# A fused attention, feed-forward and soft-MoE kernel: sign bits taken by GpSimd, the last weights loaded in whole rows, extra matmuls whose result nobody reads, and a new sequence

## The chip, the cores and the metric

The kernel runs on one core of a Trainium2 chip. The metric is the device time of one execution in microseconds (us). The core has five engines that each work through a queue of their own in order: TensorE (PE in the profile; its weight loads stand as PEld), VectorE (DVE), ScalarE (ACT), GpSimd (POOL) and SyncE (SP, which only issues transfers here). An instruction waits on semaphores for the results that it needs and for the buffer that it writes. SBUF is the memory that all engines work in, PSUM the one that matmuls write to.

## The reference

Three computations follow on one another. Only the last one's result leaves the kernel.

```python
# clustered attention: B=2, H=8, S=768, D=64, 16 clusters
q_assign = argmax(normalised q . normalised centroids); k_assign likewise
mask   = q_assign[:, :, :, None] == k_assign[:, :, None, :]
scores = where(mask, q k^T / sqrt(D), -1e9)
attn   = softmax(scores) @ v                       # as 1536 tokens x 512
# feed-forward: 512 -> 2048 -> 512
h = x @ w_in;  g = h * clip(h + 3, 0, 6) / 6;  y = g @ w_out
# soft MoE: 8 experts x 4 slots, F = 1024
logits = y @ phi
d = softmax(logits, over tokens);  slot_input = d.T @ y
slot_out[e] = maximum(slot_input[e] @ w1[e], 0) @ w2[e]     # 4 rows each
out = softmax(logits, over slots) @ slot_out                # 1536 x 512, float32
```

The feed-forward weights `w_in` and `w_out` arrive as float64; the other inputs are float32.

## The kernel before

One function holds everything. Each piece of work is a Python generator that `ev(...)` appends to a list: a piece issues a few instructions and yields. A string of numbers, `ORDER` (2,600 of them), says which generator is stepped next, and `flush` steps them in that order. This order is the program order, and so the order in every engine's queue. A second table, `ROOMS`, says for each tile name which of the buffers of its kind ("rooms") it takes. There are three PSUM rooms of two banks for scores and most other products (`pss`) and two of one bank (`psm`).

The stages, with the times of the profiled execution of before:

- **0 to 31 us, start.** Constants, centroids, and head 0: q and k are loaded, cast to a high and a low float16 half (L330 to L341) and transposed by PE (L382, tile `tq`); the other heads' transposes are made by a DMA. Then cluster assignment (`as_mm`, L428) and row maxima.
- **31 to 136 us, the eight heads of the first batch.** For each head and each of six blocks of 128 rows: scores for the row maximum (`sm`, PE L514), the maximum (`mxs`, DVE L530), scores again (`st`, PE L552 and L556), the exponential (`p`, ACT L600), its float16 halves (`pp`, ACT L331 and POOL L341) and the product with v (`acc`, PE L622 to L628). Between these stands the narrowing of the float64 weights: eight tiles of 128x1024 of `w_in` (`win`) and eight of `w_out` (`wout`).
- **136 to 320 us.** The second batch's heads, interleaved with the feed-forward of the first six token tiles (`hid`, PE L693, and `act`), its logits and the dispatch to slots.
- **320 to 405 us.** The feed-forward of the other six token tiles.
- **405 us to the end at 473.7 us.** The slots: the experts' first layer (`layer1`, PE L1324), relu, a transpose, the second layer (`layer2`, PE L1361, for experts 0 to 3, and `layer2_part`, PE L1381, for experts 4 to 7, the "last group"), `slots_out` (PE L1278), and `combine` (PE L1305, evictions L1311 and L1313), which writes the output with DMAs (L1315).

**The narrowing.** A float64 value is two 32-bit words. `narrow` builds the float32 in three parts: part 0 takes the sign bit of the high word (DVE L861, tile `nw`, one buffer) and, on ACT, the absolute value scaled (L863, tile `nt` in a `pss` room); part 1 shifts and joins both (DVE L866); part 2 joins the top bits of the low word (DVE L871). DVE and ACT have other work between these parts.

**The loads of the last phase.** `fetch` takes the entries of a list, `chunks`, one after another; each issues two or more DMAs on SP: "o" is the product `w_out` written back to memory, "1" the experts' first weights, "2" the second weights of experts 0 to 3 in halves of four row blocks, and "d" the second weights of experts 4 to 7 in column parts, `PARTS` being columns 0 to 255, 256 to 383 and 384 to 511. The column parts let the last phase run column by column: as soon as the first part's weights are there, its second layer, its `slots_out` and its `combine` can run and its output can leave, while the next part's weights load.

## Time and profile before

| | before |
|---|---|
| time, median of 3 runs | 481.71 us (479.29 to 484.8) |
| the profiled execution's own time | 475.53 us |
| its span, first to last instruction | 473.7 us |
| PE busy | 427.5 us (90% of the span) |
| ACT busy | 316.9 us (67%) |
| DVE busy | 283.1 us (60%) |
| POOL busy | 248.8 us (53%) |
| bytes moved by DMA | 95.48 MB, mean 202 GB/s |
| granted TensorE clock, mean | 0.987 |

The profiled execution is itself shorter than the three timed ones; the rows below add up to its 475.53 us, of which 1.8 us lie outside the span. A busy share of 90% for PE is a mean over stages with different limits, and PE's matmuls are pipelined with modelled ends. The chain that ended last is followed back from the last instruction, so each of its entries delayed what stands behind it. The DMA share is that of the core's 16 DMA engines, and can pass 1 where packets overlap.

### The profile page before, as it was taken

What the parts mean: (1) busy time and instruction counts of PE and PEld (TensorE: products, weight loads), DVE (VectorE), ACT (ScalarE), POOL (GpSimd) and SP (SyncE); (2) the same over time, 40 slices, a digit from 0 to 9 for tenths busy, and PEclk for the clock granted to TensorE, in tenths of its full rate; (3) what the DMA queues carried; (4) which work ended last, traced back from release to release, by engine and by line L of the source; (5) the groups of instructions that cost most, each with busy time, mean ns of one, the idle gap of its engine ahead of it and who ended that gap; (6) DMA issues with size and microseconds to landing.
All of it is one profiled execution on the core that took longest, in us unless ns stands there. A gap on an engine that the chain in (4) does not pass through costs nothing.

```text
span 473.7 us, 11606 instructions
## 1 busy us (share of the span) xinstructions
PE 427.5 (90%) x4802; PEld 271.8 (57%) x4802; DVE 283.1 (60%) x497; ACT 316.9 (67%) x518; POOL 248.8 (53%) x227
## 2 busy tenths in 40 slices
PE   2699999999979999999999998989898999889884
PEld 1357677777857466656666666654554444533353
DVE  4999999999957576375666868422244124631123
ACT  5699998899966779767889898963355336500121
POOL 4467658757534466576788897983322333030000
PEclk9999999999989999999999999999999999979999
DMA  8788959756779854584858956008998769998998
GB/s 263 212 158 213 264 102 286 167 157 229 189 242 221 182 147 86 90 136 113 179 125 127 149 119 125 1 1 135 282 412 293 167 142 342 409 396 293 345 291 274
DMA packets 133812, 95.48 MB, mean 202 GB/s; under 512 B 96384, under 2 KB 119424, under 8 KB 133760
## 3 DMA queue, kind: packets, MB, share of 16 engines
q1 hardware_dynamic: 129088, 88.95, 72.3%
q10 hardware_dynamic: 4672, 5.80, 3.5%
q8 instruction: 37, 0.61, 0.6%
q14 instruction: 15, 0.12, 0.1%
HBM read 64.06 MB, written 7.34 MB: 151 GB/s over the span
## 4 chain that ended last, share of the span: by engine, by line
PE 50%; DVE 18%; ACT 11%; DMA 8%; issue 6%; POOL 5%; DVEq 0%; ACTq 0%; SPq 0%; POOLq 0%
PE h L693 21%; DVE mxs L530 7%; PE e L1324 3%; ACT p L600 3%; PE st L552 3%; PE st L556 3%; POOL pp L341 2%; PE sm L514 2%; PE acc L622 2%; ACT pp L331 2%; POOL ghl L341 2%; DMA wk<-in_moe_w_dram 2%; DMA wod<-in_moe_w_out_dram 2%; PE z L802 1%; PE o L1361 1%
## 5 line engine op out<-in xcount | busy, mean ns | idle before, releaser
L341 POOL TENSOR_TENSOR pp<-p,pp 128x768 f16<-128x768 f32 x72 | 118.6, 1655 | 56.0 <-ACT pp L331 23.4
L693 PE MATMUL h<-wq,xt 128*128 128x512 f16 x576 | 131.6, 379 | 1.1 <-DMA xt<-xhl 1.1
L530 DVE TENSOR_REDUCE mxs<-sm 128x1 f32<-128x768 f32 x96 | 88.9, 952 | 16.5 <-PE sm L514 15.8
L693 PEld LDWEIGHTS <-xt 128*128 128x128 f16 x576 | 55.2, 98 | 62.1 <-DMA xt<-xhl 2.0
L341 POOL TENSOR_TENSOR ghl<-r,ghl 128x1024 f16<-128x1024 f32 (+1 forms) x25 | 50.3, 2012 | 61.5 <-ACT ghl L331 57.4
L600 ACT ACTIVATE p<-st 128x768 f32<-128x768 f32 x72 | 57.9, 808 | 13.2 <-PE st L556 9.8
L331 ACT ACTIVATE pp<-p 128x768 f16<-128x768 f32 x72 | 60.4, 844 | 1.2
L552 PE MATMUL st<-qk1t 128*128 128x384 f16 x192 | 48.4, 334 | 5.6 <-ACT p L600 4.0
L712 DVE SCALAR_TENSOR_TENSOR r<-r,h 128x1024 f32<-128x1024 f32 (+1 forms) x26 | 29.6, 1137 | 38.7 <-ACT r L710 38.6
L514 PE MATMUL sm<-qk2t 80*128 80x384 f16 x192 | 47.2, 339 | 4.6 <-DVE qk2t L385 1.5
L556 PE MATMUL st<-qk2t 102*128 102x384 f16 x192 | 48.7, 335 | 0.0
L710 ACT ACTIVATE r<-h,b_relu 128x1024 f32<-128x1024 f32 (+1 forms) x26 | 27.2, 1046 | 24.3 <-PE h L693 17.0
L627 PE MATMUL acc<-v,pp 128*128 128x65 f16 x432 | 36.1, 192 | 0.2 <-DVE mv L501 0.2
L622 PE MATMUL acc<-v,pp 128*128 128x65 f32 x288 | 36.2, 276 | 0.0
L628 PE MATMUL acc<-v,pp 128*128 128x64 f16 x432 | 36.1, 194 | 0.0
L622 PEld LDWEIGHTS acc<-v,pp 128*128 128x128 f32 x288 | 35.3, 195 | 1.2 <-DVE mv L501 0.3
L331 ACT ACTIVATE ghl<-r 128x1024 f16<-128x1024 f32 (+1 forms) x26 | 25.7, 988 | 14.9 <-DVE r L712 10.9
L627 PEld LDWEIGHTS <-pp 128*128 128x128 f16 x432 | 31.1, 99 | 3.3 <-DVE mv L501 0.6
L341 POOL TENSOR_TENSOR qk<-qk,qk 128x768 f16<-128x768 f32 x15 | 24.7, 1645 | 13.5 <-DMA qk<-in_q_dram 4.8
L628 PEld LDWEIGHTS <-pp 128*128 128x128 f16 x432 | 29.2, 96 | 2.7
L331 ACT ACTIVATE qk<-qk 128x768 f32<-128x768 f32 (+2 forms) x32 | 26.0, 818 | 3.7 <-DMA qk1t<-qk 2.5
L552 PEld LDWEIGHTS <-qk1t 128*128 128x128 f16 x192 | 17.3, 103 | 17.3 <-issue 11.4
(193 smaller groups left out, 756.3 us busy)
## 6 DMA issues: line engine op xcount, KB each, us to landing
wk<-in_moe_w_dram SPq DMA_DIRECT2D x60, 512.0 KB, 8.2
wi<-in_moe_w_in_dram SPq DMA_DIRECT2D x16, 512.0 KB, 6.1
wod<-in_moe_w_out_dram SPq DMA_DIRECT2D x16, 512.0 KB, 5.0
wos<-wo ACTq DMA_DIRECT2D x8, 512.0 KB, 4.3
wk<-wos SPq DMA_DIRECT2D x8, 512.0 KB, 5.5
qk<-in_q_dram SPq DMA_DIRECT2D x16, 192.0 KB, 3.3
qk<-in_k_dram SPq DMA_DIRECT2D x16, 192.0 KB, 3.4
v<-in_v_dram SPq DMA_DIRECT2D x16, 192.0 KB, 3.7
```

Source lines behind the costliest of these rows:

```text
L331: nc.scalar.activation(out, in_, AF.Copy, scale=scale)
L341: (nc.vector if e == "v" else nc.gpsimd).tensor_tensor(out=out, in0=in_, in1=hi, op=ALU.subtract)
L514: nc.tensor.matmul(s[:, j, 0:384], d["qk2t"][0:80, n, 0], d["qk2t"][0:80, 3 * j : 3 * j + 3, 1], start=True, stop=True,)
L530: nc.vector.tensor_reduce(out=mxs[i % 2][:, 96 + n : 97 + n], in_=s[:, :, 0:384], op=ALU.max, axis=AX.XY)
L552: nc.tensor.matmul(s[:, j, 0:384], d["qk1t"][:, t, 1], d["qk1t"][:, 3 * j : 3 * j + 3, 0], start=True, stop=False)
L556: nc.tensor.matmul(s[:, j, 0:384], d["qk2t"][0 : 96 + NT, t, 1], d["qk2t"][0 : 96 + NT, 3 * j : 3 * j + 3, 0], start=False, stop=True,)
L600: nc.scalar.activation(p32, s[:, :, 0:384], AF.Exp, scale=sc_exp)
L622: nc.tensor.matmul(o, p32[:, j, r * P : (r + 1) * P], d["v32"][:, t], start=(t == 0 and n == 0), stop=False)
L627: nc.tensor.matmul(o, hi, v1[:, t, 0:65], start=(t == 0 and n == 0), stop=False)
L628: nc.tensor.matmul(o[:, 0:64], hi, v1[:, t, 65:129], start=False, stop=False)
L693: nc.tensor.matmul(s[:, fb % 2], xt[:, lhs], wq[fb][:, hl, kk], start=(n == 0), stop=(n == 11))
L712: nc.vector.scalar_tensor_tensor(out=g, in0=r, scalar=6.0 * SG, in1=sf, op0=ALU.min, op1=ALU.mult)
```

## The change

1. **The sign on GpSimd.** In `narrow`, part 0's sixteen DVE instructions become POOL instructions: the high word, read as a float32, times 0.0, which is a zero with the word's sign. The `nw` tile still has one buffer. Part 1 on DVE now waits for POOL.
2. **Extra matmuls.** `keep(n, m)` makes m matmuls of 128x256 float16 from constants into a `pss` tile that is read by nobody: 77 pieces and 168 matmuls. The first 47 pieces (108 matmuls) stand in the first 164 of `ORDER`'s 2,758 steps, nine (18 matmuls) at the end of the second batch's heads, five (10) in the slot phase, and 16 (32) behind the last matmul of the output.
3. **The last group's second layer.** Of the eight row blocks (c) of experts 4 to 7, blocks 0 to 3 are loaded as ordinary "2" chunks and blocks 4 and 5 as "c" chunks, whole rows of 512 columns, and multiplied by `layer2_rows` for all three column parts. Only blocks 6 and 7 are still loaded and multiplied by column part (`layer2_part`). All in one group, the sums grow in one `psm` and one `pss` tile, `op`.
4. **Small things.** The last token tile's `pe` takes a `pss` room; `slots_out` yields between its two matmuls; and `ORDER` and `ROOMS` are new throughout. The order of the last three parts is now columns 0 to 255, 384 to 511, 256 to 383.

The tables are cut to a line.

```diff
-    "1 1 2 8 2 8 9 9 0 9 1 9 9 9 9 1 0 5 5 3 5 13 13 1 10 10 10 10 11 11 14 15 5 0 9 795 796 6 796 797 103 103 798 "
+    "9 9 8 8 15 0 0 814 15 16 16 811 831 812 805 2 808 835 12 12 12 0 0 12 16 837 816 807 16 16 7 810 8 8 10 20 11 "
...
+    def keep(n, m):
+        t = pss(f"kw_{n}")
+        for _ in range(m):
+            nc.tensor.matmul(t[:, 0, 0:256], ident16, ident.bitcast(F16), start=True, stop=True)
+        yield
...
-        pe = psm(f"pe_{t}")
+        pe = psm(f"pe_{t}") if t < NTOK - 1 else pss(f"pe_{t}")[:, 0]
...
-            nc.vector.tensor_scalar(out=s, in0=hi, scalar1=0x80000000, scalar2=None, op0=ALU.bitwise_and)
+            sf = s.bitcast(F32)
+            nc.gpsimd.tensor_scalar(out=sf, in0=hi.bitcast(F32), scalar1=0.0, scalar2=None, op0=ALU.mult)
...
-    chunks += [("d", E - 4 + j, 0) for j in range(4)] + [("d", E - 4, 1)]
+    chunks += [("2", E - 4 + j, 0) for j in range(4)]
+    chunks += [("c", E - 4, 0), ("c", E - 2, 0), ("d", 0, 0), ("d", 1, 0)]
...
+        if kind in ("c", "d"):
+
+            t = room(n, rooms[n], 2048, f"wk_{n}")
+            if kind == "c":
+                t = t.rearrange("p (j c d) -> p j c d", j=2, c=2)
+                for j in range(2):
+                    src = w2[e + j].rearrange("(p c) d -> p c d", c=8)
+                    nc.sync.dma_start(t[:, j], src[:, 4:6])
+                    wt_[kind, e + j] = t[:, j]
+                    yield
+                return
             for p, (c0, w) in enumerate(PARTS):
-                if p:
-                    np = 2 if p == 2 else 1
-                    for c in range(np):
-                        cc = slice(8 // np * c, 8 // np * (c + 1))
-                        for j in range(4):
-                            src = w2[e + j].rearrange("(p c) d -> p c d", c=8)
-                            nc.sync.dma_start(ts[j][:, p - 1, cc], src[:, cc, c0 : c0 + w])
-                            yield
+                if (p > 0) != (e > 0):
+                    continue
+                tp = t[:, 1024 * (p == 2) :][:, 0 : 8 * w].rearrange("p (c j d) -> p c j d", j=4, c=2)
+                wt_["d", p] = tp
+                for c in range(2):
+                    src = w2[E - 4 :].rearrange("e (p c) d -> c p e d", c=8)[6 + c]
+                    nc.sync.dma_start(tp[:, c], src[:, :, c0 : c0 + w])
+                    yield
             return
-        elif kind == "d":
-            src = w2[e].rearrange("(p c) d -> p c d", c=8)[:, :, 0:256]
...
     ev(consts)
+    for n in range(7):
+        ev(keep, n, 4)
...
+    for n in range(40):
+        ev(keep, 7 + n, 2)
...
+    def layer2_rows(i):
+        g = NG - 1
+        if i == 0:
+            sl["op", 0] = psm("op_0")
+            t = pss("op_1")
+            sl["op", 1], sl["op", 2] = t[:, 0], t[:, 1]
+        for c in (range(4), range(4, 6))[i]:
+            for p, (c0, w) in enumerate(PARTS):
+                for j in range(4):
+                    wr = wt_["c", E - 4 + j][:, c - 4] if i else wv("2", E - 4 + j, 0, c)
+                    nc.tensor.matmul(
+                        sl["op", p][32 * j : 32 * j + 32, 0:w], hw(g, c, j), wr[:, c0 : c0 + w], start=(c == 0), stop=False
+                    )
+            if i == 0 and c % 2:
+                yield
+        yield
+
+    def layer2_part(p):
         c0, w = PARTS[p]
-        if i == 0:
-            sl["o2", NG - 1, p] = psm(f"o2_{NG - 1}_{p}")
-        for c in range(4 * i, 4 * i + 4):
+        for c in range(6, 8):
             for j in range(4):
                 nc.tensor.matmul(
-                    sl["o2", NG - 1, p][32 * j : 32 * j + 32, 0:w],
+                    sl["op", p][32 * j : 32 * j + 32, 0:w],
                     hw(NG - 1, c, j),
-                    wv("d", E - 4 + j, p, c)[:, 0:w],
-                    start=(c == 0),
+                    wt_["d", p][:, c - 6, j],
+                    start=False,
                     stop=(c == 7),
                 )
...
+    for n in range(30):
+        ev(keep, 47 + n, 2)
...
+    for i in range(2):
+        ev(layer2_rows, i)
     for p in range(len(PARTS)):
-        for i in range(2):
-            ev(layer2_part, p, i)
+        ev(layer2_part, p)
```

How the change moves instructions, at three places. First DVE's queue of before, within the first batch's heads: the sign of the first half of the second block of `w_in` (`nw_i`) between row maxima (`mxs`), with the cluster assignment (`as`, `mx`) behind it.

```order
L530 TENSOR_REDUCE mxs_114<-sm_1_467 128x1
L530 TENSOR_REDUCE mxs_114<-sm_4_479 128x1
L861 TENSOR_SCALAR nw_i_0_484<-wi_0_305 128x1024
L530 TENSOR_REDUCE mxs_114<-sm_3_486 128x1
L530 TENSOR_REDUCE mxs_114<-sm_0_497 128x1
L530 TENSOR_REDUCE mxs_114<-sm_5_501 128x1
```

In the changed kernel this sign stands in POOL's queue (lines are shifted, L341 is L354 there), among the low halves of v, of q and k, and of the probabilities (`pp`).

```order
L354 TENSOR_TENSOR pp_1_617<-p_0_1_618,pp_1_617 128x768
L354 TENSOR_TENSOR v_2_109<-v_2_112,v_2_109 128x6x64
L881 TENSOR_SCALAR nw_i_0_751<-wi_0_439 128x1024
L354 TENSOR_TENSOR qk_4_724<-qk_659,qk_4_724 128x6x128
L354 TENSOR_TENSOR pp_3_634<-p_0_3_635,pp_3_634 128x768
L881 TENSOR_SCALAR nw_i_1_840<-wi_1_747 128x1024
L354 TENSOR_TENSOR pp_5_757<-p_0_5_758,pp_5_757 128x768
```

Behind it on DVE the instruction that waits for POOL's sign is L886, which was L866.

```order
L558 SCALAR_TENSOR_TENSOR qk2t_615<-sm_5_655,nident 6x6x128
L471 TENSOR_TENSOR as_670<-as_670,rank 128x12x16
L886 SCALAR_TENSOR_TENSOR nt_i_0_750<-nt_i_0_750,nw_i_0_751 128x1024
L474 TENSOR_REDUCE mx_3_784<-as_670 128x12
L476 TENSOR_TENSOR oh_786<-as_670,mx_3_784 128x6x2x16
L891 SCALAR_TENSOR_TENSOR wi_0_439<-wi_0_439,nt_i_0_750 128x1024
```

The sign has left DVE; the two joining steps have stayed, with two instructions of a cluster assignment between them and more such work behind.

The second place is PE's queue at the program's start. Before, it opened with the transposes of head 0's q and k.

```order
L1450 UNCONDITIONAL_BRANCH
L382 LDWEIGHTS qk_0_132
L382 MATMUL tq_155<-ident_86,qk_0_132 128x128
L382 LDWEIGHTS qk_0_132
L382 MATMUL tq_155<-ident_86,qk_0_132 128x128
```

Now 24 matmuls of `keep` stand ahead of them; these rows are the last of these and the first transposes (L401 was L382).

```order
L363 MATMUL kw_207<-ident,ident_86 128x256
L363 LDWEIGHTS ident_86
L363 MATMUL kw_210<-ident,ident_86 128x256
L363 LDWEIGHTS ident_86
L363 MATMUL kw_210<-ident,ident_86 128x256
L401 LDWEIGHTS qk_0_133
L401 MATMUL tq_214<-ident_86,qk_0_133 128x128
```

Behind the twelve transposes stand twelve more around the centroids' transpose, then the first assignment, then 28 more ahead of the second set of transposes, and 44 before head 0 is finished.

The third place is the end of SP's queue: the last group's second weights (`wk`) and the outputs. Before, the first column part was loaded in pieces of 128x4x256, the other two in pieces of 128x8x128 and 128x4x128.

```order
L1024 DMA wk_6706<-in_moe_w_dram 128x4x256
L1024 DMA wk_6708<-in_moe_w_dram 128x4x256 x2
L1024 DMA wk_6698<-in_moe_w_dram 128x1024
L1024 DMA wk_6701<-in_moe_w_dram 128x4x256
L1002 DMA wk_6713<-in_moe_w_dram 128x8x128
L1024 DMA wk_6706<-in_moe_w_dram 128x4x256
L1002 DMA wk_6714<-in_moe_w_dram 128x8x128
L1002 DMA wk_6715<-in_moe_w_dram 128x8x128
L1002 DMA wk_6716<-in_moe_w_dram 128x8x128
L1002 DMA wk_6713<-in_moe_w_dram 128x4x128
```

Now only six transfers at the very end are column parts (L1026); all ahead of them are whole rows.

```order
L1046 DMA wk_6890<-in_moe_w_dram 128x1024
L1015 DMA wk_6962<-in_moe_w_dram 128x1024
L1015 DMA wk_6898<-in_moe_w_dram 128x1024
L1015 DMA wk_6962<-in_moe_w_dram 128x1024
L1026 DMA wk_7014<-in_moe_w_dram 128x4x256 x2
L1026 DMA wk_7080<-in_moe_w_dram 128x4x128 x4
L1341 DMA out_dram<-late_w_7076 768x1x256
L1341 DMA out_dram<-late_b_6777 768x1x128
L1341 DMA out_dram<-late_gt 768x1x128
```

The bytes are the same; of the last group's four experts three quarters now come as whole rows, and SP issues 18 transfers for them where it issued 20.

## Rows read from the trace of the kernel before

**Rows 1.** The page: span, and busy time by engine.

```profile
span 473.7 us, 11606 instructions
...
PE 427.5 (90%) x4802; PEld 271.8 (57%) x4802; DVE 283.1 (60%) x497; ACT 316.9 (67%) x518; POOL 248.8 (53%) x227
```

**Rows 2.** Stretches of the span: busy us (x instructions) by engine, clock, DMA.

```profile
core 0: us, PE busy (x) PEld busy (x) DVE busy (x) ACT busy (x) POOL busy (x), PEclk, DMA share, GB/s
0.00:12.00 12.00, 2.73 (x29) 2.10 (x30) 5.77 (x19) 6.65 (x13) 5.31 (x43) 1.00 0.83 263
12.00:31.00 19.00, 13.68 (x99) 7.83 (x98) 17.65 (x31) 13.89 (x24) 9.92 (x12) 1.00 0.76 177
31.00:118.00 87.00, 83.96 (x1012) 65.40 (x1011) 83.68 (x133) 80.40 (x121) 60.99 (x40) 1.00 0.77 202
118.00:136.00 18.00, 14.92 (x190) 12.62 (x187) 13.22 (x23) 13.48 (x20) 9.60 (x7) 1.00 0.87 254
...
280.00:320.00 40.00, 35.95 (x561) 24.58 (x560) 20.56 (x38) 31.99 (x49) 33.47 (x23) 1.00 0.30 58
...
434.00:474.00 40.00, 28.69 (x376) 15.09 (x368) 9.17 (x18) 6.81 (x14) 0.00 (x0) 0.97 1.03 305
```

**Rows 3.** Chain that ended last (start, width): first, last of six signs.

```profile
16.98 0.69 DVE nw_i L861
...
114.36 0.69 DVE nw_o L861
```

**Rows 4.** The same chain: opening transposes, the longest waits for transfers.

```profile
13.44 1.45 PE tq L382 x12
...
118.86 5.44 DMA qk1t<-qk
...
127.18 7.58 DMA wod<-in_moe_w_out_dram
```

**Rows 5.** Groups by line and form: busy us, mean ns | idle before.

```profile
L341 POOL TENSOR_TENSOR pp<-p,pp 128x768 f16<-128x768 f32 x72 | 118.6, 1655 | 56.0 <-ACT pp L331 23.4 <-issue 17.5 <-PE st L556 5.8
...
L341 POOL TENSOR_TENSOR wq<-wi,wq 128x1024 f16<-128x1024 f32 x8 | 17.2, 2151 | 8.1 <-ACT wq L331 8.1
...
L861 DVE TENSOR_SCALAR nw_i<-wi 128x1024 uint32<-128x1024 uint32 x8 | 5.6, 694 | 0.1
...
L402 POOL COPY qk<-qk 128x768 f16<-128x768 f16 x1 | 0.8, 825 | 0.0
...
L300 POOL CAST ident<-ident 128x128 f16<-128x128 f32 x1 | 0.3, 291 | 0.1
```

**Rows 6.** Timeline of PE: two pairs of the same shape, 384 columns.

```profile
30.38 0.83 PE L514 MATMUL sm<-qk2t 80*128 80x384 f16 x2
...
31.70 0.49 PE L514 MATMUL sm<-qk2t 80*128 80x384 f16 x2
```

**Rows 7.** The chain again: 512-column matmuls, and the last second layer.

```profile
175.49 5.18 PE h L693 x24
...
463.41 1.95 PE o L1381 x64
```

**Rows 8.** Timeline of the end: last matmuls, and the output DMA before the last.

```profile
466.92 0.83 PE L1305 MATMUL po<-late_a,late_a 96*128 96x128 f16 x12 [0.68 <-DVE late_a L1289]
...
468.09 0.54 ACTq L1315 DMA_DIRECT2D out_dram<-late_w  x1
```

**Rows 9.** DMA packets, 405 to 420, 435 to 445, 446 to 458 us.

```profile
DMA packets 1675, 6.11 MB, mean 407 GB/s; under 512 B 190, under 2 KB 190, under 8 KB 1672
...
DMA packets 3272, 3.62 MB, mean 362 GB/s; under 512 B 111, under 2 KB 3153, under 8 KB 3271
...
DMA packets 6546, 3.60 MB, mean 300 GB/s; under 512 B 138, under 2 KB 6544, under 8 KB 6545
```

**Rows 10.** Waits in 31 to 120 us: total, times, longest.

```profile
POOL pp L341 <- ACT pp L331: 12.7, 6, 4.6
```

More of the change, by code (lines that the diff above doesn't have):

```diff
@@ L1284, in slots_out @@
             )
-        yield
+            yield
         s16 = sl["s16", p] = lt2k("a1", 1 + p, [512], F16)[:, 0:w]
@@ L1388, in layer2_part @@
         yield
[L1389 to L1392 removed]
+        if p == 0:
+            sl["o2s", NG - 1] = lt2k("w1", NG - 1, [512], F32)
+        nc.vector.tensor_copy(sl["o2s", NG - 1][:, c0 : c0 + w], sl["op", p][:, 0:w])
+    for n in range(30):
+        ev(keep, 47 + n, 2)
     ev(zsum)
```

13 lines of the change are left out of this document (1 added, 12 removed), and 333 rows, old and new, of tables (ORDER, ROOMS).

## The prediction

> **What bounds the kernel now.** I read the page first. PE is busy for 427.5 of 473.7 us, but that is a mean over stages [rows 1]. So I cut the span at the stages and read the busy time of each engine in each [rows 2]. There is no one bound. In the first 31 us PE idles 9.3 and 5.3 us, 14.6 in all, and from 12 us on DVE is the full engine (17.65 of 19). In the eight heads of the first batch, 31 to 118 us, three engines are nearly full at once: PE 83.96, DVE 83.68 and ACT 80.40 of 87, while POOL has 26 us to spare. From 118 to 136 nobody is full. In the last 40 us PE has 11 us of idle time and the transfers none (share 1.03): there the DMA rate sets the end.
>
> Then I followed the chain that ended last. In the first 75 us it runs almost wholly through DVE, and six of the sixteen signs lie on it, 4.1 us together (0.69, 0.60, 0.74, 0.69, 0.69, 0.69; the first and the last are shown) [rows 3]. At 118.86 and 127.18 it waits 5.44 and 7.58 us for transfers [rows 4]. These three things, DVE's work, the two waits and the last transfers, are what a change can win here.
>
> The start runs at half clock, though the clock column reads 1.00: a pair of 384-column matmuls takes 0.83 us at 30.38 and 0.49 at 31.70 [rows 6]. So PE stood at the 1.2 GHz level until about 31 us and at 2.4 behind it.
>
> **The change part by part**, against the profiled execution's 475.53 us. That lies 1.3% under the median of the timed runs, so the sum is multiplied by 481.71 / 475.53 = 1.013 at the end.
>
> *Price of a `keep` matmul.* 24 matmuls of 512 columns take 5.18 us, 0.216 each [rows 7]. Half the columns are 0.108 us at full clock and 0.216 at half.
>
> *The start, -0.7.* 108 `keep` matmuls stand before head 0 is finished. The first 24 fill a stretch where PE had nothing to do. If they bring the clock to its upper level early, what gains is PE work on the chain. Behind the first assignment that is the second set of twelve transposes, 1.45 us at 13.44 [rows 4]; at full clock 0.7 less. The rest of the start is DVE's. Bounds -0.7 and 0; that the matmuls themselves hold work up is a rival below.
>
> *The signs, -3.0.* DVE loses 16 instructions of 0.694 us [rows 5]. The chain holds 4.1 us of them. I count the last one (114.36) at nothing, because the two waits for transfers follow 4.5 us behind it and no sign moves those. Five are left, 3.4 us. Four of them lie in 31 to 118, where PE idles only 3.0 of 87 us [rows 2]: with DVE shorter PE becomes the bound at once. I take 3.0 for all five. Bounds 0 (PE and ACT were full anyhow) and -4.1.
>
> POOL gains 16 instructions that the trace does not show in this form. The nearest rows with one input are the copy of 768 elements at 825 ns and the cast of 128 at 291 [rows 5]; their slope is 534 / 640 = 0.83 ns per element, which gives 1.04 us for 1024. The two-input form of that size, 2.15 us [rows 5], is the upper bound. I take 1.04, since the product has one input. With 14 of the 16 in 31 to 118 POOL then works 61.0 + 14.6 = 75.6 of 87 us and is still not the bound. Its lower halves of the probabilities (`pp`) are mostly not waited for: POOL itself waits 12.7 us for ACT's `pp` there [rows 10]. The new wait is that of the joining step on DVE for POOL. Behind it in DVE's queue stand a cluster assignment and the row maxima, and PE's score rooms wait for these. I price it at nothing as long as POOL comes to the sign before DVE and ACT come to the join; the cover is the distance between them in the sequence. What it costs without cover is a rival.
>
> *The last weights, -2.2.* The second weights of experts 4 to 7 are 4 x 1024 x 512 x 4 bytes = 8.39 MB. Three stretches show what their pieces cost [rows 9]: 407 GB/s where packets average 3.6 KB (whole-row loads), 362 where they average 1.1 KB (256 columns), 300 at 550 bytes (128 columns). Before, 4.19 MB went at 362 and 4.19 at 300, 11.6 + 14.0 = 25.6 us. Now 6.29 MB go at 407, 1.05 at 362 and 1.05 at 300, 15.5 + 2.9 + 3.5 = 21.9 us. That is 3.7 us less in a stretch where the transfers are the bound. The Trainium skill, "DMA: Bandwidth & Descriptors", section Specifications, puts the smallest transfer for line rate at 512 bytes; the trace disagrees, with 300 GB/s at some 550 bytes against 407, but by the page this term would be zero and the sum below 472.3.
>
> Not all of the 3.7 us comes through. Before, the first column part was computed and stored while the others loaded. Now no part can end before the last two row blocks come. From the last of the second-layer matmuls (463.41 + 1.95 = 465.36) [rows 7] to the output transfer's issue (468.09 + 0.54) [rows 8] it is 3.3 us; with a part's eight matmuls of 256 columns, 8 x 2 x 1.95 / 64 = 0.5, it is 3.8. Meanwhile only the other parts' 3.5 us of loading fill the queues. The gap is 0.3 us by these rows and more by what a transfer needs to land. I choose 1.5, between 0.3 and 3.7, so -2.2. Bounds -3.4 and 0.
>
> *The other `keep` matmuls, +0.5.* Eighteen stand at the end of the second batch: 1.9 us, where PE idles 4.05 of 40 [rows 2], nothing. Ten stand in the slot phase, 1.1 us, in part on the path: +0.5. 32 stand behind PE's last output matmul, which ends at 467.75 [rows 8]: 3.5 us at full clock and 6.9 at half, ending at 471.2 or 474.7, against the span's 473.7. Nothing to +1.0; I take nothing, since the output transfers cover it.
>
> *The rest, 0.* The room of `pe_11` and the yield in `slots_out` take no work away. The new sequence keeps the order of stages, of the loads from memory and of the heads; what it does inside a stage no row prices. I take 0, and 5 us to either side as bounds, somewhat under half of the two waits in [rows 4].
>
> Sum: -0.7 - 3.0 - 2.2 + 0.5 = -5.4, so 470.1 us for a profiled execution and 470.1 x 1.013 = 476.2 on the median's scale, 1.1% faster.
>
> **The rivals.**
>
> *One half does not come.* Either the size of the packets costs nothing at the end, because something else than the rate of the transfers sets it (the rule of the Trainium skill's page named above would have it so), and the tail term is 0: 472.3, on the median's scale 478.5, chance 0.11. Or PE and ACT, full as DVE was, take up what DVE gives: 473.1, so 479.2, also 0.11. Against the first speak the three rates of [rows 9] and a transfer share of 1.03. For the second speaks that PE idles only 3 us in 87; against it that the chain of the first 75 us hardly leaves DVE.
>
> *The sequence shortens the waits at 118 to 136.* They are 13.0 us on the chain, the largest single thing there, and POOL, DVE and ACT idle beside them. If the loads that they wait for are issued some 5 us earlier: 465.1, so 471.1. For it: the transfers have room, with a share of 0.77 before the waits. Against it: the order of loads is nearly the old one.
>
> *GpSimd is late, and the kernel slower.* POOL works in order, and a sign can stand behind a `pp` (1.655 us) or a low half of a weight (2.151) [rows 5] that itself waits for ACT. DVE then waits at the join with all the maxima behind it. If the sign comes later than DVE wants it by L, each of the six places changes by L - 0.69. With L = 2.15 they cost 6 x 1.46 = +8.8 in place of -3.0: 481.9, so 488.1. The gain of all else is eaten from L = 1.09 on (6 x 0.40 = 2.4). For it: POOL at 87% of its time. Against it: the idle time of POOL before `pp` says that it mostly waits for others.
>
> *The extra matmuls hold up the start.* At half clock 108 of them take 23.3 us, and PE has 14.6 idle up to 31 us [rows 2]. If the clock does not rise, the head's own work stands 8.7 us behind them: 470.1 + 0.7 + 8.7 = 479.5, so 485.7. At full clock they take 11.7 and fit. Against it: the idle time is longest ahead of the transposes, where the first 24 stand.
>
> **How the numbers follow.** The forecast (all terms as taken, 472 to 481) has a chance of 0.40, one half missing 0.22, the shorter waits 0.15, GpSimd late 0.13, a held-up start 0.10. About 1%, 476.9 to 486.5 us, is what a measurement of this kernel can tell from no change; its own three runs spread over 1.1%. The forecast lies at that edge: 0.29 of its 0.40 below. Of the missing half 0.08 below and 0.14 within. The waits 0.15 below. GpSimd late 0.10 above and 0.03 within, the start 0.08 above and 0.02 within, if its cost or L is a little larger. Faster 0.52, same 0.30, slower 0.18. For the range: the terms at their lower bounds give 475.5 - 0.7 - 4.1 - 3.4 = 467.3, so 473.4, and with the waits 5 us shorter 468.3; spread of runs to 466. Upwards it takes in most of the two slow cases, to 487.
>
> **What would show it.** Start: the pair of 384-column matmuls at full clock well before 31 us, and the second transposes at some 0.7 us. Signs: their POOL line near 1.04 us, no wait of the join on POOL in DVE's list, and the last head of the first batch done some 3 us sooner, near 115 us. Tail: no stretch under 362 GB/s before the last 2 MB, a DMA hole of 1 to 2 us ahead of the first output. I am wrong if DVE's waits name POOL's sign for more than 1 us a time, if PE's matmuls of `keep` lie on the chain, or if the two waits at 118 us have grown by what was won before them.

## The result, and the profile after

The changed kernel takes 485.19 us (median of 18 runs, 481.91 to 490.75) against 479.9 for the kernel before (18 runs, 476.04 to 486.51). The ratio is 1.0147, with a 95% interval of 1.012 to 1.0173: 1.5% slower, where 1.1% faster was forecast. Every ratio here is taken from fast runs alone, while the medians hold all runs, so it is not the quotient of the two medians (1.011 here). The profiled execution takes 487.91 us. It is 12.4 us longer than that of before, more than the medians differ, because the profiled execution of before (475.53) is faster than any of its 18 runs; so below, sizes are taken from ratios, and places from the traces.

The page of after, its span and the busy time by engine, the answer to [rows 1]:

```profile
span 486.1 us, 11948 instructions
...
PE 450.0 (93%) x4970; PEld 290.6 (60%) x4970; DVE 273.2 (56%) x481; ACT 318.2 (65%) x518; POOL 292.4 (60%) x243
```

PE works 22.5 us more, and `keep` alone takes 27.5 (its group stands below). POOL works 43.6 us more.

The stretches of after, columns as in [rows 2], the last one to the end of the span:

```profile
12.00:31.00 19.00, 15.58 (x152) 10.93 (x150) 17.02 (x30) 13.08 (x24) 11.98 (x13) 0.91 0.75 154
31.00:118.00 87.00, 79.35 (x894) 62.09 (x894) 72.19 (x116) 71.92 (x107) 75.63 (x44) 0.93 0.70 178
118.00:136.00 18.00, 17.03 (x170) 12.60 (x169) 13.33 (x20) 15.32 (x22) 17.20 (x10) 0.88 0.63 190
...
280.00:320.00 40.00, 37.93 (x582) 27.20 (x580) 24.93 (x51) 35.77 (x59) 34.14 (x24) 1.00 0.38 62
...
434.00:486.10 52.10, 43.73 (x498) 22.00 (x498) 12.93 (x27) 7.94 (x16) 1.63 (x12) 0.99 0.87 315
```

In 31 to 118 us PE, DVE and ACT each do less than before (79.35, 72.19 and 71.92 us against 83.96, 83.68 and 80.40), and POOL does more (75.63 against 60.99). From 118 to 136 POOL is full, 17.20 of 18 us. Something holds the other three up while POOL works. The granted TensorE clock is lower too, 0.93 and 0.88 in these two stretches where before has 1.00 in both; how much of the loss comes by the clock and how much by the waits themselves, these rows do not part.

The groups of after by line and form (busy us, mean ns | idle before and its releaser), the answer to [rows 5]:

```profile
L363 PE MATMUL kw<-ident,ident 128*128 128x256 f16 x168 | 27.5, 305 | 3.9 <-POOL ident L313 1.8 <-ACT late_gt L1339 0.9 <-DVE wi L891 0.5
...
L881 POOL TENSOR_SCALAR nw_o<-wod 128x1024 f32<-128x1024 f32 x8 | 22.9, 2868 | 7.2 <-PE st L575 3.4 <-DMA wod<-in_moe_w_out_dram 3.3 <-DVE nt_i L886 0.5
L881 POOL TENSOR_SCALAR nw_i<-wi 128x1024 f32<-128x1024 f32 x8 | 22.9, 2859 | 5.1 <-DMA wi<-in_moe_w_in_dram 4.3 <-DVE nt_i L886 0.7
```

A sign takes 2.86 us on POOL. The prediction's price was 1.04 and its upper bound 2.15. The sixteen together are 45.8 us where 16.6 had been counted.

The waits of after, over the whole span (us in total, times, longest):

```profile
DVE nt_o L886 <- POOL nw_o L881: 7.9, 5, 4.4
...
DVE nt_i L886 <- POOL nw_i L881: 1.8, 2, 1.1
```

The joins on DVE now wait for POOL's sign, seven times, up to 4.4 us. The chain that ended last (start, width) shows how that goes on through the program:

```profile
74.74 2.84 POOL nw_i L881
...
90.27 7.27 DMA qk2t<-qk
...
106.36 2.47 POOL nw_i L881
...
132.52 2.85 POOL nw_o L881
...
138.91 5.65 DMA wod<-in_moe_w_out_dram
...
149.16 2.87 POOL nw_o L881
```

Before, DVE carried the chain here [rows 3]. Now POOL's signs lie on it at 2.5 to 2.9 us each (entries may hold two neighbours), down to 152 us. The wait for `w_out` that stood at 127.18 [rows 4] is still there, at 138.91. The one for `qk1t` at 118.86 is gone, and one of 7.27 us for the transposed q and k of another head (`qk2t`) stands at 90.27, where the chain of before has none. It does not come from the dear sign: a_two, with a cheap sign, has 7.39 us of it at 84.57, and a_plain, with DVE's signs, 7.56 at 90.75. The first feed-forward matmul on the chain of before and the first of the experts' first layer:

```profile
155.70 4.06 PE h L693 x18
...
422.93 12.20 PE e L1324 x96
```

The same two places on the chain of after:

```profile
163.54 6.60 PE h L712 x30
...
434.00 3.74 PE e L1350 x32
```

At the first feed-forward matmul the changed kernel is 7.8 us late, at the slot phase 11.1, at the end 12.4.

What the prediction had asked the profile to show at the start did come. The q and k transposes of after, on PE's timeline:

```profile
6.85 1.15 PE L401 MATMUL tq<-ident,qk 128*128 128x128 f16 x12
...
14.25 0.83 PE L401 MATMUL tq<-ident,qk 128*128 128x128 f16 x12 [1.05 <-ACT qk L488]
```

The second set takes 0.83 us where it took 1.45 [rows 4], so PE is at its upper level by 14 us; before, it was at the lower one until some 31 us [rows 6]. The clock column of 12 to 31 us, 0.91 in the mean, has it fall again for a part.

The end of after, in stretches of 5 us:

```profile
460.00:465.00 5.00, 3.88 (x90) 2.91 (x88) 0.32 (x1) 0.00 (x0) 0.00 (x0) 1.00 1.06 367
465.00:470.00 5.00, 4.29 (x64) 2.50 (x57) 0.89 (x2) 0.25 (x1) 0.00 (x0) 1.00 0.76 209
470.00:475.00 5.00, 3.62 (x50) 2.44 (x50) 2.80 (x6) 2.77 (x6) 0.00 (x0) 1.00 0.31 108
475.00:480.00 5.00, 3.48 (x36) 2.56 (x36) 2.82 (x7) 1.85 (x5) 0.00 (x0) 1.00 0.99 317
```

The weights come in at 367 GB/s and more until 465 us, and then the share of the transfers falls to 0.76 and 0.31 before the outputs fill them again. Two of the prediction's signs of being wrong have come: DVE's waits for POOL's sign, above, and, in a small way, `keep` on the chain. Two pairs of its matmuls lie there among the last outputs, 0.22 us each; the last 26, from 480.33 us, run beside the last output transfer.

### The profile page after: what moved, and what is told of

Same layout as the page of the kernel before. It is cut to its first block, busy times and chain, and to the rows that moved or that the text cites. A ratio compares the mean times of both kernels' runs of the same rounds, so it can differ in the third digit from the quotient of the medians.

```text
span 486.1 us, 11948 instructions
## 1 busy us (share of the span) xinstructions
PE 450.0 (93%) x4970; PEld 290.6 (60%) x4970; DVE 273.2 (56%) x481; ACT 318.2 (65%) x518; POOL 292.4 (60%) x243
## 4 chain that ended last, share of the span: by engine, by line
PE 51%; DMA 12%; POOL 11%; ACT 8%; DVE 6%; issue 5%; ACTq 0%; SPq 0%; POOLq 0%; DVEq 0%
PE h L712 24%; DMA wk<-in_moe_w_dram 6%; DMA qk2t<-qk 4%; POOL pp L354 4%; PE sm L533 3%; PE st L571 3%; POOL nw_o L881 2%; PE st L575 2%; ACT p L619 2%; ACT pp L344 2%; POOL nw_i L881 2%; PE acc L654 2%; PE z L821 2%; PE acc L641 2%; PE acc L646 1%
## 5 line engine op out<-in xcount | busy, mean ns | idle before, releaser
L712 PE MATMUL h<-wq,xt 128*128 128x512 f16 x576 | 133.6, 382 | 0.0
L354 POOL TENSOR_TENSOR pp<-p,pp 128x768 f16<-128x768 f32 x72 | 118.4, 1650 | 23.7 <-ACT pp L344 10.9
L354 POOL TENSOR_TENSOR ghl<-r,ghl 128x1024 f16<-128x1024 f32 (+1 forms) x25 | 50.4, 2017 | 68.9 <-ACT ghl L344 58.7
L619 ACT ACTIVATE p<-st 128x768 f32<-128x768 f32 x72 | 58.2, 810 | 18.4 <-PE st L575 12.6
L533 PE MATMUL sm<-qk2t 80*128 80x384 f16 x192 | 46.2, 336 | 8.5 <-DMA qk2t<-qk 5.2
L646 PEld LDWEIGHTS <-pp 128*128 128x128 f16 x432 | 32.1, 101 | 4.2 <-issue 1.6
L647 PEld LDWEIGHTS <-pp 128*128 128x128 f16 x432 | 30.0, 97 | 2.8 <-issue 0.3
L363 PE MATMUL kw<-ident,ident 128*128 128x256 f16 x168 | 27.5, 305 | 3.9 <-POOL ident L313 1.8
L354 POOL TENSOR_TENSOR qk<-qk,qk 128x768 f16<-128x768 f32 x15 | 24.9, 1660 | 10.1 <-ACT qk L344 8.0
L533 PEld LDWEIGHTS <-qk2t 80*128 80x128 f16 x192 | 17.1, 100 | 21.2 <-DMA qk2t<-qk 6.7
```

Of the source, the lines that this page charges most:

```text
L354: (nc.vector if e == "v" else nc.gpsimd).tensor_tensor(out=out, in0=in_, in1=hi, op=ALU.subtract)
L533: nc.tensor.matmul(s[:, j, 0:384], d["qk2t"][0:80, n, 0], d["qk2t"][0:80, 3 * j : 3 * j + 3, 1], start=True, stop=True,)
L619: nc.scalar.activation(p32, s[:, :, 0:384], AF.Exp, scale=sc_exp)
L646: nc.tensor.matmul(o, hi, v1[:, t, 0:65], start=(t == 0 and n == 0), stop=False)
L647: nc.tensor.matmul(o[:, 0:64], hi, v1[:, t, 65:129], start=False, stop=False)
L712: nc.tensor.matmul(s[:, fb % 2], xt[:, lhs], wq[fb][:, hl, kk], start=(n == 0), stop=(n == 11))
```

## The experiments

Each kernel is the kernel before or the changed kernel with one or two edits. Ratios are to the kernel before, run beside it on the same chip, with their 95% intervals. Not all kernels ran on the same chip, so small differences between two rows are less sure than the ratios. 0.01 of a ratio is 4.8 us.

| kernel | sequence | sign | extra matmuls | whole row blocks | median us (runs) | ratio |
|---|---|---|---|---|---|---|
| changed | new | POOL, 1 scalar | 168 | 6 | 485.19 (18) | 1.0147 (1.012 to 1.0173) |
| a_dve | new | DVE | 168 | 6 | 486.46 (4) | 1.0116 (1.0041 to 1.0191) |
| a_nokeep | new | POOL, 1 scalar | none | 6 | 488.16 (4) | 1.0113 (1.0017 to 1.021) |
| a_four | new | POOL, 1 scalar | 168 | 4 | 486.74 (10) | 1.0112 (1.0071 to 1.0153) |
| a_plain | new | DVE | none | 4 | 484.7 (7) | 1.0119 (1.0089 to 1.0149) |
| b_pool | old | POOL, 1 scalar | none | column parts | 497.08 (4) | 1.0311 (1.0242 to 1.0379) |
| b_two | old | POOL, 2 scalars | none | column parts | 481.83 (12) | 1.0035 (0.9994 to 1.0075) |
| b_tail | old | DVE | none | 6 | 482.7 (12) | 1.0063 (1.0034 to 1.0092) |
| b_keep | old | DVE | 64 | column parts | 475.8 (12) | 0.9937 (0.9912 to 0.9962) |
| b_keep_short | old | DVE | 64, narrow | column parts | 475.41 (6) | 0.9887 (0.984 to 0.9933) |
| b_keep_two | old | POOL, 2 scalars | 64 | column parts | 482.65 (12) | 1.007 (1.0029 to 1.0112) |
| a_two | new | POOL, 2 scalars | 168 | 6 | 473.9 (6) | 0.9851 (0.9801 to 0.9901) |
| a_two_four | new | POOL, 2 scalars | 168 | 4 | 473.33 (6) | 0.9863 (0.9799 to 0.9926) |
| a_two_start | new | POOL, 2 scalars | 108 | 6 | 474.8 (12) | 0.9935 (0.9894 to 0.9976) |
| a_two_nokeep | new | POOL, 2 scalars | none | 6 | 475.76 (12) | 0.9956 (0.9916 to 0.9996) |

**The theories.** The first: POOL's sign is dear, and every join behind it waits. Its rivals: the extra matmuls hold the path up; the new sequence is worse by itself; the new tail costs what the whole rows win. The first four runs undo or do one part each.

**a_dve: the signs back on DVE, in the changed kernel.**

```diff
-            nc.gpsimd.tensor_scalar(out=sf, in0=hi.bitcast(F32), scalar1=0.0, scalar2=None, op0=ALU.mult)
+            nc.vector.tensor_scalar(out=s, in0=hi, scalar1=0x80000000, scalar2=None, op0=ALU.bitwise_and)
```

> The changed kernel with the sixteen signs back on DVE (bitwise and), all else as changed. If GpSimd's signs (2.86 us each in the trace, on the chain from 45 to 152 us) are the cause of the loss of the first 155 us, the milestones there come back to within 2 us of before (they are 8 to 11 us late), and the ratio falls from 1.0147 to between 0.992 and 1.000; what is left is the tail, some 4 us. If the extra matmuls or the new sequence are the cause, the ratio stays between 1.010 and 1.018.

Measured: 1.0116. By the first theory it should have fallen to 1.000 or less; it lies in the range that was set for the rivals. So the first theory is not enough: with DVE's signs, too, the changed kernel is slower than before. One reason shows in the trace, since in the new sequence the signs cost DVE more than in the old. The groups by line and form of a_dve:

```profile
L880 DVE TENSOR_SCALAR nw_i<-wi 128x1024 uint32<-128x1024 uint32 x8 | 8.4, 1054 | 0.1
...
L880 DVE TENSOR_SCALAR nw_o<-wod 128x1024 uint32<-128x1024 uint32 x8 | 7.4, 924 | 3.8 <-DMA wod<-in_moe_w_out_dram 3.7
```

One of these signs on the chain of a_dve (start, width):

```profile
75.06 2.12 DVE nw_i L880
```

POOL's timeline of a_dve at that time:

```profile
74.46 2.16 POOL L354 TENSOR_TENSOR wq<-wi,wq 128x1024 f16<-128x1024 f32 x1 [1.35 <-ACT wq L344]
```

The same instruction that took 0.694 us [rows 5] takes 1.05 and 0.92 in the mean. The one at 75.06 takes 2.12 us and stands beside a POOL instruction with two inputs that runs from 74.46 to 76.62. The timelines of all sixteen bear this out: nine signs take 0.82 to 2.12 us, and each of the nine begins while such a POOL instruction runs; the four that meet none take 0.68, two that begin before one 0.69 and 0.70, and one that begins 0.1 us before the end of one 0.69. The Trainium skill, "GPSIMD Engine Reference", section 1, Specifications, says that GpSimd's SBUF interfaces are shared with VectorE and contended by some of VectorE's instructions. These rows agree, but no run here takes the POOL instructions away to prove it.

**b_pool: the sign on POOL alone, in the kernel before** (the same line, the other way round).

> The kernel before with nothing changed but the sixteen signs, which POOL takes as a product with zero, at the places where DVE took them. If POOL's signs are the cause: each 2.8 to 2.9 us, 45 us more on POOL, and a ratio of 1.015 to 1.03 (the sequence of before leaves no room for them). If the cost of the form comes only with the new sequence: each near 1.04 us and a ratio under 1.005.

Measured: 1.0311, some 15 us. The groups by line and form of b_pool:

```profile
L862 POOL TENSOR_SCALAR nw_i<-wi 128x1024 f32<-128x1024 f32 x8 | 22.9, 2866 | 2.9 <-DVE nt_i L867 2.9
L862 POOL TENSOR_SCALAR nw_o<-wod 128x1024 f32<-128x1024 f32 x8 | 22.8, 2855 | 3.0 <-DMA wod<-in_moe_w_out_dram 1.6 <-DVE nt_i L867 1.4
```

The waits of b_pool over the whole span (total, times, longest):

```profile
DVE nt_o L867 <- POOL nw_o L862: 14.9, 7, 4.0
...
DVE nt_i L867 <- POOL nw_i L862: 3.5, 2, 2.9
```

The price is 2.86 us in this sequence too, and the joins wait 18.4 us for it. The sign on POOL in this form is by far the dearest part of the change. The new sequence takes most of that up: with it the same signs cost 0.3% more than DVE's (1.0147 against 1.0116, intervals that overlap), with the old one 3.1%.

**a_nokeep: the changed kernel without the extra matmuls.**

```diff
-        for _ in range(m):
+        for _ in range(0 if True else m):
             nc.tensor.matmul(t[:, 0, 0:256], ident16, ident.bitcast(F16), start=True, stop=True)
```

> The changed kernel without the 168 extra matmuls (the tiles are still taken, nothing is issued). If these hold up the path, the ratio falls to 1.005 or less. If POOL's signs are the cause, it stays at 1.010 to 1.020, and the start is at half clock until some 30 us again, so that the second transposes take 1.45 us.

Measured: 1.0113, inside the range of the first theory, with a wide interval. No sign, then, that the extra matmuls make the kernel slower; a_two_nokeep below says the same more sharply. The transposes are at half clock again (a median of 0.311 us each, 0.220 with the extra matmuls in b_keep below).

**a_four: four row blocks by column part in place of two.** Blocks 4 and 5 join blocks 6 and 7 in the column parts; the loads in `fetch` are split to match.

```diff
...
-        for c in (range(4), range(4, 6))[i]:
+        for c in (range(4), ())[i]:
...
-        for c in range(6, 8):
+        for c in range(4, 8):
```

> The changed kernel with four row blocks (4 to 7) of the last group loaded by column part instead of two (6 and 7); the bytes are the same, 2.1 MB fewer come in whole rows. If the loss of the tail is the time in which no output can leave and little is left to load (the DMA share falls to 0.31 in 470 to 475 us), the second half of the loads covers it: the hole shrinks from some 5 us to 2 or less and the time falls by 2 to 3 us, a ratio of 1.008 to 1.011. If the rate of the loads decides, it rises by 1 to 2 us, to 1.016 to 1.019.

Measured: 1.0112, at the edge of what the hole (the time ahead of the first output in which the transfers have little to carry) would give; the interval reaches to 1.0153. It points to the hole but does not show it.

**b_tail: the new second layer of the last group alone, in the kernel before.** The code of the changed tail, in the old sequence, with the loads at the places of the old ones.

> The kernel before with the new second layer of the last group alone (whole rows but for row blocks 6 and 7), signs on DVE, no extra matmuls, the sequence of before. By the prediction's term the tail gains 2.2 us: ratio 0.995. If the hole costs what the changed kernel's trace shows (last weights about 3.5 us sooner, but no output until all are in, some 6 us more from the last landing to the end), it loses 1 to 4 us: 1.002 to 1.009.

Measured: 1.0063, a loss of 3.0 us. The end of b_tail in stretches of 5 us:

```profile
455.00:460.00 5.00, 3.41 (x84) 2.61 (x76) 0.00 (x0) 0.00 (x0) 0.00 (x0) 1.00 0.91 236
460.00:465.00 5.00, 3.56 (x43) 2.39 (x42) 2.29 (x5) 2.03 (x4) 0.00 (x0) 1.00 0.02 5
465.00:470.00 5.00, 4.32 (x41) 3.28 (x40) 2.94 (x6) 1.77 (x5) 0.00 (x0) 0.60 0.61 213
```

The loads end near 460 us, and then the transfers do nothing for 5 us and little for the next 2 (shares 0.91, 0.02, 0.61). Before, they were busy to 470 us. The shares missing from 1 in these three stretches are 1.46 x 5 = 7.3 us of idle transfers, against 1.5 in the prediction. Not all of the 3.0 us need be the tail's own cost in the changed kernel. In the old sequence the twelve transposes of `cTp` stand between the last products and the first output (460.12 to 460.96 us), and the granted clock is down to 0.60 from 465 us on; the first part's weights, issued at 446.47 with 10.7 us to landing, are in 8.0 us before the first output's issue at 465.16. In the changed kernel these transposes stand at 448 us, the clock is 1.00 up to 480 us, and the way is 4.4 us (467.75 to 472.17). There the lateness grows from 11.1 us at the slot phase to 12.4 at the end, 1.3 us.

**b_keep: 64 extra matmuls at the start alone, in the kernel before.** `keep` is defined as in the changed kernel, and its sixteen pieces stand among the first 41 steps of `ORDER`; all other steps are the old ones.

```diff
+    for n in range(16):
+        ev(keep, n, 4)
```

> The kernel before with 64 extra matmuls at the start alone (24 ahead of the first transposes, 12 behind them, 28 behind the first assignment). By the prediction's term the clock is up before 10 us and the second transposes take 0.8 us where they took 1.45: ratio 0.998 to 1.000. If they hold up the start: the first row maximum later than 18.7 us and a ratio above 1.004.

Measured: 0.9937, a gain of 3.0 us where 0.7 had been forecast at the best. **b_keep_short** is the same with 16 columns:

```diff
-            nc.tensor.matmul(t[:, 0, 0:256], ident16, ident.bitcast(F16), start=True, stop=True)
+            nc.tensor.matmul(t[:, 0, 0:16], ident16, ident.bitcast(F16)[:, 0:16], start=True, stop=True)
```

> The kernel before with the same 64 extra matmuls at the start, at the same places, but of 16 columns in place of 256. If the gain of 0.6% comes from the clock that the extra work brings up, it is gone: 0.998 to 1.002, and the clock rises near 29 us as before. If it comes from the shift of what follows in the queues: 0.992 to 0.996 again.

Measured: 0.9887. The transposes stay at half clock, and the gain stays too. So the gain is not the clock that these transposes get. PE's transposes in b_keep (count: least/median/most ns):

```profile
L394 PE MATMUL tq<-ident,qk x24: 218/220/220, 6.7 to 15.8; 128*128 128x128 f16 x24
```

The same in b_keep_short:

```profile
L394 PE MATMUL tq<-ident,qk x24: 262/311/314, 5.3 to 15.7; 128*128 128x128 f16 x24
```

The stretch from 118 to 156 us in before (columns as in [rows 2]):

```profile
118.00:156.00 38.00, 33.17 (x375) 26.43 (x372) 28.70 (x47) 29.28 (x44) 17.25 (x13) 0.96 0.87 216
```

The same stretch in b_keep:

```profile
118.00:156.00 38.00, 35.75 (x417) 27.83 (x414) 31.27 (x50) 31.25 (x48) 19.69 (x14) 1.00 0.82 240
```

And in b_keep_short:

```profile
118.00:156.00 38.00, 36.19 (x422) 28.29 (x419) 31.88 (x51) 32.14 (x48) 19.69 (x14) 1.00 0.83 245
```

Here PE, DVE and ACT do 2 to 3 us more work in the same stretch, at a clock of 1.00 where before has 0.96. In 110 to 140 us ACT and DVE wait 4.3 and 3.8 us for `w_out` in before, 2.2 and 2.0 in b_keep. This names a place and not the whole gain: the span of b_keep_short's profiled execution is 473.8 us, that of before's 473.7, and the gain stands in the timed runs alone. Which of the 64 matmuls shifts the waits, and whether the waits or the clock behind them earn it, stays open.

**a_plain: the new sequence with nearly nothing else** (signs on DVE, no extra matmuls, four blocks by column part; the three edits above together).

> The changed kernel's sequence and rooms, but signs on DVE, no extra matmuls, and four row blocks by column part: what is left is nearly the new sequence alone. If the sequence itself costs time (transposed q and k of the next head late, DVE waiting for scores), the ratio is 1.006 to 1.013. If the signs, the extra matmuls and the tail share the loss, it is 1.003 or less.

Measured: 1.0119. The new sequence loses 1.2% when DVE takes the signs, with or without the rest (a_dve, 1.0116). So the sequence is not good for any kernel. That it suits signs on POOL, if they are cheap, a_two below shows. What it loses with DVE's signs is not shown in full: the chain of a_plain has the 7.56 us for `qk2t` at 90.75, and signs of up to 2.13 us, but no run takes either away.

**b_price: what the instruction costs.** Six forms on POOL, ahead of the first two signs; the sign itself stays on DVE, so only the durations count.

```diff
+                g.tensor_scalar(out=sf, in0=hi.bitcast(F32), scalar1=0.0, scalar2=None, op0=ALU.mult)
+                g.tensor_scalar(out=sf, in0=sf, scalar1=0.0, scalar2=None, op0=ALU.mult)
+                g.tensor_scalar(out=sf[:, 0:512], in0=sf[:, 0:512], scalar1=0.0, scalar2=None, op0=ALU.mult)
+                g.tensor_scalar(out=sf, in0=sf, scalar1=0.0, scalar2=0.0, op0=ALU.mult, op1=ALU.add)
+                g.tensor_copy(sf, sf)
+                g.tensor_copy(sf, hi.bitcast(F32))
```

> The kernel before with twelve extra GpSimd instructions ahead of the first two signs, for their durations alone: a product with one scalar reading every second word (the sign's form), the same read and written without gaps, over 512 elements, with two scalars, and plain copies without and with gaps. If the gaps cost it: 2.86 us with and near 1.04 without. If the product with a scalar costs it: 2.86 for both, and copies near 1.04.

POOL's timeline in b_price (start, width):

```profile
11.63 2.84 POOL L864 TENSOR_SCALAR nw_i<-wi 128x1024 f32<-128x1024 f32 x1
14.55 2.77 POOL L865 TENSOR_SCALAR nw_i<-nw_i 128x1024 f32<-128x1024 f32 x1
17.40 1.49 POOL L866 TENSOR_SCALAR nw_i<-nw_i 128x512 f32<-128x512 f32 x1
18.97 1.04 POOL L867 TENSOR_SCALAR nw_i<-nw_i 128x1024 f32<-128x1024 f32 x1
20.08 1.04 POOL L868 COPY nw_i<-nw_i 128x1024 f32<-128x1024 f32 x1
21.18 1.10 POOL L869 COPY nw_i<-wi 128x1024 f32<-128x1024 f32 x1
```

The gaps cost next to nothing (2.84 against 2.77, 1.10 against 1.04). What costs is the form with one scalar: 2.77 us, 2.5 ns per element by the difference to 512 elements (1.28 us), against 1.04 us for the form with two scalars, which does more arithmetic, and for a copy. The prediction's 1.04 is the price of the second form.

**a_two: the changed kernel with the two-scalar form.** -0.0 is added so that the sign of the zero stays.

```diff
-            nc.gpsimd.tensor_scalar(out=sf, in0=hi.bitcast(F32), scalar1=0.0, scalar2=None, op0=ALU.mult)
+            nc.gpsimd.tensor_scalar(out=sf, in0=hi.bitcast(F32), scalar1=0.0, scalar2=-0.0, op0=ALU.mult, op1=ALU.add)
```

> The changed kernel with the sign taken by GpSimd in the form with two scalars (times 0.0, plus -0.0), which took 1.04 us where the form with one took 2.8. Signs 1.04 to 1.10 us each and 29 us less on POOL. If POOL's load is what the new sequence suffers from: ratio 0.995 to 1.004. If the sequence costs its 1.2% whatever takes the signs (as with DVE, 1.0116): 1.007 to 1.012.

Measured: 0.9851, 473.9 us: 1.5% faster than before and 3% faster than the changed kernel, from two operands of one line. The groups by line and form of a_two:

```profile
L881 POOL TENSOR_SCALAR nw_o<-wod 128x1024 f32<-128x1024 f32 x8 | 9.2, 1149 | 9.4 <-DMA wod<-in_moe_w_out_dram 3.7 <-PE st L575 3.1 <-PE acc L654 1.3
L881 POOL TENSOR_SCALAR nw_i<-wi 128x1024 f32<-128x1024 f32 x8 | 9.1, 1143 | 6.1 <-DMA wi<-in_moe_w_in_dram 5.2 <-DVE nt_i L886 0.9
```

The stretch from 31 to 118 us of a_two:

```profile
31.00:118.00 87.00, 82.35 (x974) 64.73 (x972) 77.16 (x122) 77.85 (x116) 70.44 (x49) 0.98 0.77 198
```

The joins' wait for POOL (in after 7.9 us in five waits and 1.8 in two) is this in a_two:

```profile
DVE nt_o L886 <- POOL nw_o L881: 0.2, 1, 0.2
```

The three other kernels with this sign and the new sequence have one longer wait each, 4.7 to 5.2 us, and in them POOL itself waits 8.1 to 8.8 us for the loads of `w_out`. The signs take 1.15 us (a copy with gaps took 1.10). POOL has 5 us less to do in this stretch than in after, and PE, DVE and ACT each get 3 to 6 us more done there. Since nothing but the form of the sign differs, its price is shown to be worth these 3%.

**b_two: the same cheap signs in the sequence of before.**

> The kernel before with the signs on GpSimd in the two-scalar form alone. This is the prediction's term at the prediction's price of 1.04 us: by it -3.0 us, ratio 0.991 to 0.996. If DVE's relief is worth nothing because PE and ACT are full: 0.998 to 1.003. If the order of POOL's queue makes the joins wait at any price: above 1.005 (1.031 with the one-scalar form).

Measured: 1.0035, between 0.9994 and 1.0075. Near the prediction's price (1.13 us each) the signs win nothing in the old sequence. The joins still wait for POOL 6.3 us (5.2 in four waits and 1.1 in one). **b_keep_two** adds the 64 matmuls of b_keep:

> The kernel before with the 64 extra matmuls at the start (0.9937 alone) and GpSimd's signs in the two-scalar form. If both add up: 0.985 to 0.991. If the signs bring nothing: 0.992 to 0.996.

Measured: 1.007. The two edits by themselves would multiply to 0.9972 (0.9937 x 1.0035), which lies under the interval of the two together (1.0029 to 1.0112). So effects of this size do not add here; why not, no row settles.

**The other edits, with the sign mended.** a_two_four, a_two_start (n from 47 on issues nothing) and a_two_nokeep are a_two with the edits shown above.

> The changed kernel with the two-scalar sign and four row blocks of the last group by column part instead of two. If the hole ahead of the first output is a cost of its own (four blocks gained 0.3% with the dear sign): 0.978 to 0.984, and the DMA share of the 5 us behind the last weights above 0.6. If the rate of the loads is worth as much as the hole: 0.984 to 0.990.

Measured: 0.9863, between 0.9799 and 0.9926: no difference to a_two can be told. In the trace the hole is much smaller, though. One stretch of a_two:

```profile
455.00:460.00 5.00, 4.05 (x42) 2.30 (x42) 2.60 (x5) 2.15 (x4) 0.00 (x0) 1.00 0.23 65
```

The same stretch of a_two_four:

```profile
455.00:460.00 5.00, 3.93 (x72) 2.62 (x70) 2.45 (x5) 2.75 (x5) 0.00 (x0) 1.00 0.82 245
```

The share rises from 0.23 to 0.82, and neither the span (473.6 and 473.2 us) nor the time moves. Why is not shown. In these two traces the way from the first matmul of the experts' first layer to the end is 52.4 and 50.9 us, so that this part is 1.5 us shorter with four blocks; but the matmul itself begins at 421.2 and 422.3, 1.1 us later.

> The changed kernel with the two-scalar sign and no extra matmuls. If they earn something by the clock: 0.987 to 0.993. If they are worth nothing or cost: 0.981 to 0.986.

Measured: 0.9956, beyond the upper range: the extra matmuls earn something, if the two ratios from different chips may be compared (0.9851 with them; the intervals do not meet).

> The changed kernel with the two-scalar sign and the extra matmuls of the start alone (108 of 168; the 60 later ones are not issued). If the later ones cost (they stand in the slot phase and among the outputs): 0.980 to 0.984. If they are hidden: 0.984 to 0.987, as with all of them.

Measured: 0.9935, the opposite of what was expected if the later ones cost. With the 60 later ones it is 0.9851. The intervals touch, and the two were not run side by side; by the medians, 474.8 and 473.9 us, the difference is 0.2%. On the same chip, a_two_four with all 168 is at 0.9863, and its interval overlaps that of a_two_start. So this is likely at most, and not shown. The traces name a place, the slot phase, in the stretch from 420 to 434 us. First a_two:

```profile
420.00:434.00 14.00, 13.62 (x128) 4.63 (x131) 4.17 (x11) 1.12 (x2) 2.67 (x20) 1.00 1.02 379
```

Then a_two_nokeep:

```profile
420.00:434.00 14.00, 13.62 (x113) 4.31 (x116) 3.05 (x8) 1.12 (x2) 2.44 (x18) 0.88 0.98 358
```

And a_two_start:

```profile
420.00:434.00 14.00, 12.74 (x104) 4.21 (x100) 1.58 (x4) 0.60 (x1) 3.63 (x25) 0.88 0.97 359
```

Without the later matmuls the granted clock falls to the lower level for part of this stretch (0.88 in the mean), as it does in before (0.80 to 0.86 from 410 to 430); with them it stays at 1.00, also in a_two_four. The median granted clock of the runs is 0.996 in a_two, 0.986 in a_two_nokeep and 0.981 in a_two_start.

## Why the prediction was wrong, point by point

**The price of the sign is the step that failed.** The text took 1.04 us, "since the product has one input", and 2.15 as the upper bound. It is 2.86. The two rows under the 1.04 were a copy and a cast; no row of before shows a product with one scalar. The bound came from an instruction with two inputs, and a row with one input was taken to lie under it. It does not. With the price wrong, POOL's load, and the sentence that the new wait costs nothing, fell with it: seven signs in 31 to 118 us took 20.0 us of POOL. That POOL's load there came out at 75.63 us where 75.6 had been forecast is luck. The text put 14 of the 16 signs into this stretch; in before nine lie there, in after seven, so that too many signs at too low a price made up the sum, and `pp` and the rest of POOL did less. The sign of being wrong that belongs to this step, DVE's waits for POOL's sign above 1 us a time, came (up to 4.4 us).

**The rival that came true is "GpSimd is late".** It had 0.13, and a price of 488.1; 485.19 was measured. Its reason was off: it had the signs late because they stand behind a `pp` or a `wq`. They stand there in a_two as well, in the same order, and with 1.15 us in place of 2.86 the joins' waits fall from 9.7 us to 0.2. Its place, the joins on DVE, is what the waits show.

**With the price that was forecast, the forecast time comes.** a_two is at 0.9851, and 476.2 us was forecast; a_two has 473.9. But this is not the sum being right. Taken apart in the old sequence, the terms are: signs +1.7 us (0.0035, with an interval that takes in 0) at the cheap price, where -3.0 stood; the tail +3.0, where -2.2 stood; the start -3.0, where -0.7 stood, and not by the clock. They add up to +1.7 us, and a_two gained some 7. So the near hit is luck: what made the gain was the new sequence together with the cheap sign, and the sum had the sequence at 0.

**The sequence was set to 0 and is what binds it all.** Its bounds of 5 us to either side were about right: +5.7 with DVE's signs (a_plain), and with cheap signs and no extra matmuls some 4 us better than the old one (a_two_nokeep 0.9956, which has the new tail as well, b_two 1.0035; the intervals just overlap). The prediction costed it apart from the sign. It had to be costed with it: the sequence puts work between sign and join, and a_two against the changed kernel shows that what it needs is a short sign. Which of its moves earn the gain stays open.

**The tail.** The loads did come 3 to 4 us sooner and at 400 GB/s; that half of the term stands, and the rates of the whole rows fit it, as the three of [rows 9] have them. The 512 bytes that the Trainium skill, "DMA: Bandwidth & Descriptors", section Specifications, names as the smallest transfer for line rate would have left that half at nothing. These runs disagree, with 410 GB/s in after from 445 to 460 us, where whole rows are loaded, against 300 at some 550 bytes [rows 9]. The gap of 1.5 us was mis-sized: 7.3 us of idle transfers in b_tail, 4.7 in after ((1 - 0.76 + 1 - 0.31) x 5). Two things were left out. When the first part is in, little of the others is left to load: from 467.75 to 472.17 us in after the transfers move 62 GB/s at a share of 0.23, so the 3.5 us of other loads cover next to nothing. And from the landing of the first part to its first output the way is longer than 3.8 us: two products, three evictions and the issue, from 467.79 to past 472.17 us in after. What the tail costs in the changed kernel was not run with its own sequence; 1.3 us by the chain, as said under b_tail.

**The extra matmuls.** That they bring the clock up early is right (0.83 us for the transposes, seen). That this would earn 0.7 us is neither shown nor needed; b_keep_short had the gain with the transposes at half clock. The +0.5 for the later ones had the wrong sign, as far as the runs tell: they keep the clock up in the slot phase.

## What to carry to other kernels

Before an instruction is moved to another engine, find a row of the very form, operation and operand kinds, on that engine; where there is none, time the form alone, and do not bound it by another form that seems heavier. A sequence that was laid out for one set of durations is worth its gain only with them: the same changed kernel was 1.5% faster with a sign of 1.15 us and 1.5% slower with one of 2.86. And a load that becomes faster by delaying the first result must pay for the time in which the queues then have nothing to carry.

## What the runs showed of the hardware

- GpSimd's product with one scalar takes 2.77 us for 128x1024 float32 words without gaps, and the form with two scalars 1.04 (b_price).
- A VectorE instruction of 0.69 us took 0.82 to 2.12 us in the nine cases of a_dve in which it began while a GpSimd instruction with two inputs was running, and 0.68 in the four in which none ran beside it; the cause was not tested apart.
- The granted clock fell for part of 420 to 434 us in a_two_nokeep and a_two_start (0.88 in the mean), in which PE had been busy 13.62 and 12.74 of 14 us, and not in a_two, which has the same work and a few more matmuls.
